# Reordering the expert layer of an attention + two-layer expert kernel: six product blocks in one stretch, weight splits one group later

## The chip, the cores and the metric

The kernel runs on one core of a Trainium2 chip. The time is the device time of one execution in microseconds (us), the median of several. The engines are TensorE (PE, with its weight loads shown as PEld), VectorE (DVE), ScalarE (ACT), GpSimd (POOL) and SyncE (SP), which here only starts transfers. Each engine works through its own queue in program order; between engines there are semaphores.

## The reference

```python
x = attention(q, k, v)                 # 2 x 8 heads x 576 x 64; window masks -> 1152 x 512
h = x @ w_in                           # 512 -> 2048
x = (h * tanh(softplus(h))) @ w_out    # 2048 -> 512
p = domain_probs / (domain_probs.sum(-1, keepdims=True) + 1e-9)
out = 0
for e in range(4):                     # 1152 tokens, w1[e] 512 x 1024, w2[e] 1024 x 512
    out += p[:, e:e+1] * (np.maximum(x @ w1[e], 0) @ w2[e])
```

Everything is float32. The kernel keeps that accuracy by splitting each operand into a high part (rounded to the format in which PE multiplies fast) and a low part (the rest): a product is three matmuls, high x high, high x low and low x high. Each split is therefore one ACT instruction (the high part) and one DVE or POOL instruction (the low part, source minus high).

## The kernel before

**Up to the second expert layer.** The attention runs over ten units of up to 128 rows (class `Unit`): transposes, scores, softmax, values, transposes back. `idle` matmuls at the very start (`NWARM`, L250) keep PE at work before the first k arrives. The weights of the first layer are loaded in halves of 512 KB by `dec_load` and split by `dec_dve` and `dec_act`, from step 6 of the attention on. Class `Step1` is the first layer; its 16 x 2 + 16 steps alternate first and second products and fill PE from about 55 us on.

**The second expert layer** works on 32 groups (class `Group`): 4 experts e, two sets of columns j (j = 0: 2 x 256 tokens, j = 1: 2 x 320 tokens), 4 pairs p of 128-wide slices of the hidden dimension; p runs fastest, then j, then e. A group's first product x @ w1 is done as a 2 x 2 block product with seven block products in place of eight (a Strassen scheme): A11·B11, S1·T1, A12·B21, S2·T2, S4·B22, S3·T3 and A22·T4. Each is six matmuls (`prod`, L788). They accumulate in three PSUM banks a, b, c. Between them lie copies and sums, since a bank is used on: p1 (ACT copies a after A11), c22 (ACT copies b after S1), u2 (ACT copies a after S2), then on DVE c11 = c + p1, c12 = b + u2, c22 = a + c22 (after S3), and the relu splits: `relu_split(0, ...)` of c11 and c12, `relu_split(1, ...)` of c22, and after A22, which uses bank a again, the split of c21 from PSUM. The second product (`second(f)`, f = 0 and 1) of a group is done during the next group: 4 (j = 0) or 5 (j = 1) rows of 128 tokens, three matmuls of 512 columns each per f, accumulated over p in banks 1 to 5. After p = 3 `finish` (L871) has DVE scale each row by the probability and add it to `scr`; for the last expert each row goes out by a transfer.

**Order in a group i before.** For j = 0: A11, S1, A12, S2, S4; `second(0)` of group i-1; slot (i, 0); S3; `second(1)` and `finish` of group i-1; A22; slot (i, 1). For j = 1: A11, S1, S2, A12, S3; `second(0)`; slot (i, 0); S4, A22; `second(1)` and `finish`; slot (i, 1). In j = 0 the banks a and c change places with every p, so that A22 of one group and A12 of the next use the same bank; in j = 1 they do not.

**The slots** (dictionary `slots`, L998) hold the preparation of weights: `prep_a(n)` (L735: two splits of the staged w1 of pair n, then four sums on POOL in place), `prep_s(n)` (L744: the split of these sums, then the load of w1 of pair n+1 into the same buffer), `prep_w2(n)` (L759: high part of w2 on ACT, low part on POOL, then the load of w2 of pair n+1). For experts 1 to 3 they stand like this, g being a j = 1 group except for p = 3, where it is the first group of the next expert (groups 8, 16, 24):

```python
n, g = e * NP2 + p, 2 * NP2 * (e - 1) + NP2 + p + 1
slots.setdefault((g, 0), []).append(lambda n=n: prep_a(n))
slots.setdefault((g, 1), []).append(lambda n=n: prep_s(n))
slots.setdefault((g + 1, 0) if p == NP2 - 1 else (g, 1), []).append(lambda n=n: prep_w2(n))
```

For expert 0 slots (1, 0) to (3, 1) hold the last pairs and the block sums and splits of the second set's columns (`set1_b`, `set1_sums`, `set1_t`), T2 in (3, 1).

**The tail** (L1029): the second product of the last group, row by row; its last row is cut into two halves of 256 columns in the same bank, and both are finished after the last matmul.

Of the kernel before, what the change touches and what calls it, by code (L numbers as in the profile page):

```python
# [14 lines left out]
AF = mybir.ActivationFunctionType  # L15
ALU = mybir.AluOpType
# [7 lines left out]
def kernel(  # L24
# [13 lines left out]
    PE, ACT, DVE, POOL, SP = nc.tensor, nc.scalar, nc.vector, nc.gpsimd, nc.sync  # L38
# [3 lines left out]
    DM = out.shape[1]  # L42
# [27 lines left out]
    def bank(n):  # L70
        return ps.tile([128, 512], F32, tag=f"bank{n}", name=nm("bank"))
# [177 lines left out]

    t = bank(7)  # L250
    for n in range(NWARM):
        PE.matmul(t, warm, warm4, start=n == 0, stop=n == NWARM - 1)

# [200 lines left out]

    u0.transposes()
    load(u4.load_k, u4.load_q, *vq[2:4], *vd_loads(0, 2))
# [46 lines left out]
    u0.x_hi()  # L503
    u0.x_lo()
    u2.probsT()
    u4.transposes()
    vq = vp_loads(1, 0, 2)
# [3 lines left out]
    def att_step(s):  # L511
        n2, n1, u, p1, p2 = (au[n] for n in (s + 2, s + 1, s, s - 1, s - 2))
        dec = s >= DEC0
        p1.probsT_copy()
        if s > DEC0:
            dec_act()
        if not dec:
            copy_v(n1.c)
        n1.spread()
        u.scores()  # L520
        u.softmax()
        p1.sums()
        p1.values()
        p2.xT()
        p1.normalise()
        p2.x_hi()
        if dec:
            dec_dve()
            copy_v(n1.c)
        p2.x_lo()  # L530
        n2.transposes([0])
        if s == 3:
            u.probsT()
        n2.transposes([1])
        if s != 3:
            u.probsT()

        if s == 4:
            load(au[9].load_k, *vq[0:2], au[9].load_q, *vq[2:4])
        elif s == 5:  # L540
            load(dec_load, *vd_loads(1, 2), dec_load, *vd_loads(1, 3), *vp_loads(1, 4, NCH), *vd_loads(1, 4))
        elif s == 6:
            dec_load()

# [224 lines left out]
    class Group:  # L769
# [25 lines left out]

        def first_a(self):
            assert ("s", self.e * NP2 + self.p) in ready
            N = self.N
            self.a, self.b, self.c = (bank(m)[:, 0:N] for m in ((0, 7, 6) if self.apart and self.p % 2 else (6, 7, 0)))
            self.cb = rawf[2][:, 0:3 * N]  # L800
            p1, u2 = (late[4][:, 320 * i:320 * i + N] for i in range(2))
            self.u2 = u2
            self.prod(self.a, "A11", "B11", True)
            self.prod(self.b, "S1", "T1", True)
            ACT.activation(p1, self.a, AF.Copy)  # L805
            ACT.activation(self.cb[:, 2 * N:3 * N], self.b, AF.Copy)
            if self.apart:
                self.prod(self.c, "A12", "B21", True)
                self.prod(self.a, "S2", "T2")
                self.prod(self.b, "S4", "B22")  # L810
                DVE.tensor_tensor(out=self.cb[:, 0:N], in0=self.c, in1=p1, op=ALU.add)
                ACT.activation(u2, self.a, AF.Copy)
                DVE.tensor_tensor(out=self.cb[:, N:2 * N], in0=self.b, in1=u2, op=ALU.add)
                self.relu_split(0, slice(0, 2 * N), self.cb[:, 0:2 * N])
                return
            self.prod(self.a, "S2", "T2")
            self.prod(self.c, "A12", "B21", True)
            ACT.activation(u2, self.a, AF.Copy)
            self.prod(self.a, "S3", "T3")
            DVE.tensor_tensor(out=self.cb[:, 0:N], in0=self.c, in1=p1, op=ALU.add)  # L820
            self.c22()

        def c22(self):
            o = slice(2 * self.N, 3 * self.N)
            DVE.tensor_tensor(out=self.cb[:, o], in0=self.a, in1=self.cb[:, o], op=ALU.add)

# [4 lines left out]

        def mid(self):
            N = self.N
            self.relu_split(1, slice(N, 2 * N), self.cb[:, 2 * N:3 * N])

        def first_u3(self):
            self.prod(self.a, "S3", "T3")
            self.c22()
            self.mid()

        def first_c21(self):
            self.prod(self.a, "A22", "T4")
            self.relu_split(1, slice(0, self.N), self.a)

        def first_b(self):
            N = self.N
            self.prod(self.b, "S4", "B22")
            self.prod(self.a, "A22", "T4")
            DVE.tensor_tensor(out=self.cb[:, N:2 * N], in0=self.b, in1=self.u2, op=ALU.add)
            self.relu_split(1, slice(0, N), self.a)  # L850
            self.relu_split(0, slice(0, 2 * N), self.cb[:, 0:2 * N])

# [6 lines left out]

        def second(self, f, which=slice(None)):  # L860
            assert ("w2", self.e * NP2 + self.p) in ready
            wh, wl = (w[:, 512 * f:512 * f + 512] for w in pair_w2(self.p))
            hi, lo = self.g[f]
            for acc, t, cols in self.accs()[which]:
                s = slice(128 * t, 128 * t + 128)
                for i, (x, a) in enumerate(((hi, wh), (hi, wl), (lo, wh))):
                    PE.matmul(acc, x[:, s], a[:, cols], start=self.p == 0 and f == 0 and i == 0,  # L867
                              stop=self.p == NP2 - 1 and f == 1 and i == 2,
                              skip_group_check=self.n >= NG2 - NP2 and t == self.rows - 1)
# [122 lines left out]
    for e in range(NE):  # L992
        for j in range(2):
            for p in range(NP2):
# [4 lines left out]
             (2, 0): [lambda: set1_b(2), lambda: set1_sums(0), lambda: prep_w2(3)], (2, 1): [lambda: set1_sums(1), lambda: set1_t("T1")],  # L999
             (3, 0): [lambda: set1_t("T3"), lambda: set1_t("T4")], (3, 1): [lambda: set1_t("T2")]}  # L1000
    for e in range(1, NE):
# [5 lines left out]
    for i, g in enumerate(groups):  # L1007
        before = groups[i - 1] if i else None
        g.first_a()
        if before:  # L1010
            before.second(0)
        else:
            steps[NS1 - 1].second(units_at=[0])
        if not g.apart:
            g.mid()
        for do in slots.get((i, 0), ()):
            do()
        g.first_u3() if g.apart else g.first_b()
        if before:
            before.second(1)  # L1020
            before.finish()
        else:
            steps[NS1 - 1].second(units_at=[1])
            y_out(2)
        if g.apart:
            g.first_c21()
        for do in slots.get((i, 1), ()):
            do()
    g = groups[-1]  # L1029
    accs = g.accs()  # L1030
    acc, t, _ = accs.pop()
    accs += [(acc[:, c], t, c) for c in (slice(0, DM // 2), slice(DM // 2, DM))]
    for t in range(len(accs)):
        for f in range(2):
            g.second(f, slice(t, t + 1))
        if t < len(accs) - 2:
            g.finish(slice(t, t + 1))
    g.finish(slice(len(accs) - 2, len(accs)))

# [31 lines left out]
```

## Time and profile before

| | |
|---|---|
| median of 3 runs | 629.46 us (628.78 to 629.7) |
| profiled execution | 629.2 us, of which the trace's span is 627.4 us |
| PE busy | 619.6 us, 99% of the span |
| PEld | 556.9 us, 89% |
| DVE, ACT, POOL busy | 289.1, 262.3, 181.0 us |
| granted TensorE clock | 1.00 in all stretches |
| second expert layer | from about 247 us to the end |

Busy time of PE is not PE at its peak: matmuls are pipelined and each record is longer than the distance to the next one. The distances between the starts, or the chain of work that ended last, tell the pitch. Times of rows below are microseconds from the start of the span.

### The profile page before, as it was taken

Reading aid. Unit: us, or ns where it says so; the run is one execution under the profiler, and the core shown is the slowest. Engines: PE = TensorE matmul, PEld = TensorE weight load, DVE = VectorE, ACT = ScalarE, POOL = GpSimd, SP = SyncE. Lnnn points to the kernel's source line nnn. Section 1 sums busy time; section 2 is a strip of 40 time slices with the busy share of each in tenths; the row PEclk is TensorE's granted clock in tenths of the full one; section 3 lists DMA queues with packets and bytes.
Section 4 is the critical chain, followed back from the end, with each engine's and each line's share of the span. In section 5 each row is a group of like instructions: output and inputs, shape, how many; then the busy total and the mean of one; then the engine's idle time right before and its main releaser. Section 6 shows DMA issues by size and latency. Waiting matters only on the chain.

```text
span 627.4 us, 10147 instructions
## 1 busy us (share of the span) xinstructions
PE 619.6 (99%) x4152; PEld 556.9 (89%) x4152; DVE 289.1 (46%) x482; ACT 262.3 (42%) x497; POOL 181.0 (29%) x201
## 2 busy tenths in 40 slices
PE   8999999999999999999999999999999999999997
PEld 5777888889999999998998999998989988989986
DVE  6898787614112343474544523444524444434223
ACT  7787777623223443452434322444322443322220
POOL 8854555502000241280244200334200335100000
PEclk9999999999999999999999999999999999999999
DMA  8875776300000122030022200122200122001002
GB/s 191 206 197 171 233 228 209 101 1 1 1 1 1 68 85 83 1 102 1 23 81 99 67 1 1 34 87 82 68 1 0 34 102 68 1 1 40 28 1 84
DMA packets 51358, 43.66 MB, mean 70 GB/s; under 512 B 26352, under 2 KB 44144, under 8 KB 51312
## 3 DMA queue, kind: packets, MB, share of 16 engines
q1 hardware_dynamic: 51312, 43.02, 22.8%
q8 instruction: 32, 0.52, 0.4%
q14 instruction: 14, 0.11, 0.1%
HBM read 40.65 MB, written 2.36 MB: 69 GB/s over the span
## 4 chain that ended last, share of the span: by engine, by line
PE 91%; DMA 3%; POOL 2%; SPq 1%; DVE 1%; ACT 1%; issue 0%; DVEq 0%; POOLq 0%; ACTq 0%
PE bank L867 31%; PE bank L793 28%; PE bank L593 16%; PE bank L569 15%; DMA raw<-in_moe_w_out_dram 1%; SPq L285 1%; POOL vD L294 1%; DMA natk<-in_k_dram 1%; DMA scr<-in_moe_w_in_dram 1%; POOL vP L292 1%; DMA vD<-in_v_dram 0%; SPq L316 0%; DMA vP<-in_v_dram 0%; POOL vD L207 0%; POOL vP L206 0%
## 5 line engine op out<-in xcount | busy, mean ns | idle before, releaser
L793 PE MATMUL bank<-xh,late 128*128 128x256 f32 (+1 forms) x512 | 118.0, 293 | 0.0
L793 PE MATMUL bank<-wxh,late 128*128 128x320 f32 (+1 forms) x384 | 93.4, 294 | 0.0
L793 PEld LDWEIGHTS bank<-xh,late 128*128 128x128 f32 x512 | 87.9, 188 | 1.8
L867 PE MATMUL bank<-late,gh 128*128 128x512 f32 x280 | 87.0, 392 | 0.0
L739 POOL TENSOR_TENSOR raw<-raw 128x256 f32<-128x256 f32 x16 | 12.3, 767 | 222.4 <-DVE late L621 222.4
L569 PE MATMUL bank<-xh,late 128*128 128x320 f32 (+1 forms) x288 | 75.9, 336 | 0.0
L793 PE MATMUL bank<-xl,late 128*128 128x256 f32 (+1 forms) x256 | 74.7, 292 | 0.0
L593 PE MATMUL bank<-gh,late 128*128 128x320 f32 (+1 forms) x288 | 72.0, 336 | 0.0
L793 PEld LDWEIGHTS bank<-wxh,late 128*128 128x128 f32 x384 | 67.8, 188 | 0.9 <-ACT late L805 0.3
L578 DVE TENSOR_TENSOR gl<-scr,gh 128x512 fp32r<-128x512 f32 (+1 forms) x32 | 24.5, 766 | 81.0 <-ACT gh L577 81.0
L867 PEld LDWEIGHTS bank<-late,gh 128*128 128x128 f32 x280 | 50.9, 188 | 9.0
L574 ACT ACTIVATE scr<-bank 128x320 f32<-128x320 f32 (+1 forms) x48 | 23.5, 489 | 82.2 <-PE bank L569 82.1
L755 POOL TENSOR_TENSOR late<-raw,late 128x1024 fp32r<-128x1024 f32 x16 | 38.8, 2425 | 64.0 <-ACT late L751 64.0
L793 PE MATMUL bank<-wxl,late 128*128 128x256 f32 (+1 forms) x192 | 56.2, 293 | 0.1
L867 PE MATMUL bank<-late,gl 128*128 128x512 f32 x140 | 54.5, 389 | 0.0
L569 PEld LDWEIGHTS bank<-xh,late 128*128 128x128 f32 x288 | 50.7, 188 | 3.8
L593 PEld LDWEIGHTS bank<-gh,late 128*128 128x128 f32 x288 | 50.0, 188 | 3.7
L867 PE MATMUL bank<-late,late 128*128 128x512 f32 (+1 forms) x219 | 52.8, 388 | 0.0
L793 PEld LDWEIGHTS bank<-xl,late 128*128 128x128 f32 x256 | 48.1, 188 | 1.7
L569 PE MATMUL bank<-xl,late 128*128 128x320 f32 (+1 forms) x144 | 48.4, 336 | 0.0
L593 PE MATMUL bank<-gl,late 128*128 128x320 f32 (+1 forms) x144 | 48.4, 336 | 0.0
L867 PE MATMUL bank<-late,wxh 128*128 128x512 f32 (+1 forms) x154 | 47.3, 389 | 0.0
(153 smaller groups left out, 1135.9 us busy)
## 6 DMA issues: line engine op xcount, KB each, us to landing
raw<-in_moe_w_dram SPq DMA_DIRECT2D x32, 512.0 KB, 3.5
raw<-in_moe_w_out_dram SPq DMA_DIRECT2D x15, 512.0 KB, 3.8
raw<-in_moe_w_in_dram SPq DMA_DIRECT2D x9, 512.0 KB, 4.2
scr<-in_moe_w_in_dram SPq DMA_DIRECT2D x7, 512.0 KB, 4.5
natk<-in_k_dram SPq DMA_DIRECT2D x8, 256.0 KB, 3.4
natq<-in_q_dram SPq DMA_DIRECT2D x8, 256.0 KB, 4.0
out_dram<-scr SPq DMA_DIRECT2D x8, 256.0 KB, 2.0
vD<-in_v_dram SPq DMA_DIRECT2D x16, 64.0 KB, 3.8
```

The lines of the kernel that those rows point to most:

```text
L285: SP.dma_start(out=job[0], in_=job[1])
L292: POOL.tensor_copy(vP[before, :, g0:g1, j, :], vP[own, :, g0 - 1:g1 - 1, j, :])
L294: POOL.tensor_copy(vD[before, :, j, c, :], vD[own, :, j, c - 1, :])
L569: PE.matmul(h, a[:, c, :], x[:, c, :], start=c == 0 and k == 0, stop=c == 3 and k == 2)
L574: ACT.activation(self.hc[:, self.w * i:self.w * (i + 1)], h, AF.Mish)
L578: DVE.tensor_tensor(out=self.glo, in0=self.hc, in1=self.ghi.bitcast(F32), op=ALU.subtract)
L593: PE.matmul(yacc[self.grp][d], a[:, 512 + 128 * d:640 + 128 * d], x[:, g], start=u == UORD[self.grp][0] and k == 0, stop=u == UORD[self.gr ...
L739: POOL.tensor_tensor(out=a22, in0=a21, in1=a22, op=ALU.add)
L755: POOL.tensor_tensor(out=lo, in0=stage2, in1=hi.bitcast(F32), op=ALU.subtract)
L793: PE.matmul(out, w, x(k), start=first and k == 0 and i == 0, stop=k == 1 and i == 2, skip_group_check=not first)
L867: PE.matmul(acc, x[:, s], a[:, cols], start=self.p == 0 and f == 0 and i == 0, stop=self.p == NP2 - 1 and f == 1 and i == 2, skip_group_ch ...
```

## The change

One stretch of PE work per group, for both sets: A11, S1, (A12, S2 or S2, A12), S4, S3, then both halves of the second product of the group before with slot (i, 0) issued between them, then `finish`, then A22. In both sets the banks a and c now change places with p. The slot (i-1, 1), which stood at the end of group i-1, is issued within `first` of group i: after its PE work, the copies and the sums c11 and c12, and before its relu splits. T2 goes to slot (3, 0), T4 to (3, 1). The second half of the very last row accumulates in a bank of its own (bank 6): what had been accumulated for it before the last group is scaled and added to `scr` by one more DVE operation. At the start there are a shorter idle product more and one between the transposes of the first unit; the first transposes of unit 4 come before the probabilities of unit 2; one load of weights is issued in attention step 5 and not in step 6.

```diff
-    u0.transposes()
+    u0.transposes([0])
+    idle_product()
+    u0.transposes([1])
...
+    u4.transposes([0])
     u2.probsT()
-    u4.transposes()
+    u4.transposes([1])
...
-            load(dec_load, *vd_loads(1, 2), dec_load, *vd_loads(1, 3), *vp_loads(1, 4, NCH), *vd_loads(1, 4))
-        elif s == 6:
-            dec_load()
+            load(dec_load, *vd_loads(1, 2), dec_load, *vd_loads(1, 3), dec_load, *vp_loads(1, 4, NCH), *vd_loads(1, 4))
...
-        def first_a(self):
+        def first(self, between):
             assert ("s", self.e * NP2 + self.p) in ready
             N = self.N
-            self.a, self.b, self.c = (bank(m)[:, 0:N] for m in ((0, 7, 6) if self.apart and self.p % 2 else (6, 7, 0)))
+            self.a, self.b, self.c = (bank(m)[:, 0:N] for m in ((0, 7, 6) if self.p % 2 else (6, 7, 0)))
...
             ACT.activation(u2, self.a, AF.Copy)
+            DVE.tensor_tensor(out=c11, in0=self.c, in1=p1, op=ALU.add)
+            self.prod(self.b, "S4", "B22")
+            DVE.tensor_tensor(out=c12, in0=self.b, in1=u2, op=ALU.add)
             self.prod(self.a, "S3", "T3")
+            for do in between:
+                do()
+            self.relu_split(0, slice(0, 2 * N), cb[:, 0:2 * N])
+            DVE.tensor_tensor(out=c22, in0=self.a, in1=c22, op=ALU.add)
+            self.relu_split(1, slice(N, 2 * N), c22)
...
-             (3, 0): [lambda: set1_t("T3"), lambda: set1_t("T4")], (3, 1): [lambda: set1_t("T2")]}
+             (3, 0): [lambda: set1_t("T2"), lambda: set1_t("T3")], (3, 1): [lambda: set1_t("T4")]}
...
-        g.first_a()
+        g.first(slots.get((i - 1, 1), ()))
         if before:
             before.second(0)
...
-        if not g.apart:
-            g.mid()
         for do in slots.get((i, 0), ()):
             do()
-        g.first_u3() if g.apart else g.first_b()
         if before:
             before.second(1)
             before.finish()
...
-        if g.apart:
-            g.first_c21()
-        for do in slots.get((i, 1), ()):
-            do()
+        g.first_c21()
...
-    accs += [(acc[:, c], t, c) for c in (slice(0, DM // 2), slice(DM // 2, DM))]
+    half = [slice(0, DM // 2), slice(DM // 2, DM)]
+    row = g.row0 + t
+    o = scr[:, DM * row:DM * (row + 1)][:, half[1]]
+    DVE.scalar_tensor_tensor(out=o, in0=acc[:, half[1]], scalar=prob[:, row, g.e:g.e + 1], in1=o,
+                             op0=ALU.mult, op1=ALU.add)
+    accs += [(acc[:, half[0]], t, half[0]), (bank(6)[:, half[1]], t, half[1])]
     for t in range(len(accs)):
         for f in range(2):
-            g.second(f, slice(t, t + 1))
-        if t < len(accs) - 2:
-            g.finish(slice(t, t + 1))
-    g.finish(slice(len(accs) - 2, len(accs)))
+            g.second(f, slice(t, t + 1), fresh=t == len(accs) - 1)
+        g.finish(slice(t, t + 1))
```

## Rows read from the trace of the kernel before

**Rows 1.** The page, chain that ended last: share of the span by engine.

```profile
PE 91%; DMA 3%; POOL 2%; SPq 1%; DVE 1%; ACT 1%; issue 0%; DVEq 0%; POOLq 0%; ACTq 0%
```

**Rows 2.** The chain in order of time, second expert layer: start, length, what, matmuls.

```profile
298.54 4.38 PE bank L793 x30
...
348.42 4.10 PE bank L793 x36
352.53 2.74 PE bank L867 x12
355.27 0.70 PE bank L793 x6
```

**Rows 3.** Waits of PE's weight loads: us in total, times, longest us.

```profile
PEld bank L793 <- DVE wxl L621: 0.3, 1, 0.3
PEld bank L793 <- ACT late L805: 0.3, 1, 0.3
```

**Rows 4.** Timeline near the end: last matmul of A22, its relu split; last rows.

```profile
613.19 0.31 PE L793 MATMUL bank<-wxh,late 128*128 128x320 f32 x1
...
613.53 0.44 ACT L829 ACTIVATE late<-bank 128x320 fp32r<-128x320 f32 x1 [4.11 <-PE bank L793]
...
614.00 0.49 DVE L830 SCALAR_TENSOR_TENSOR late<-bank,late 128x320 fp32r<-128x320 f32 x1 [0.85 <-ACT late L829]
...
623.83 0.88 DVE L881 SCALAR_TENSOR_TENSOR scr<-bank,prob,scr 128x256 f32<-128x256 f32 x2 [0.68 <-PE bank L867]
```

**Rows 5.** Timeline at the end of the attention: DVE takes up the moved load.

```profile
47.69 0.66 DVE L155 TENSOR_SCALAR scr<-scr 128x512 uint32<-128x512 uint32 x1 [0.23 <-POOL wxl L180]
```

**Rows 6.** Timeline of group 9 (S2, u2), and of group 28, where PE waited.

```profile
361.86 0.28 PE L793 MATMUL bank<-wxh,late 128*128 128x256 f32 x1
...
362.17 0.38 ACT L812 ACTIVATE late<-bank 128x256 f32<-128x256 f32 x1 [0.98 <-PE bank L793]
...
362.54 0.30 PEld L867 LDWEIGHTS bank<-late,wxh 128*128 128x128 f32 x2
...
567.38 0.44 ACT L805 ACTIVATE late<-bank 128x320 f32<-128x320 f32 x1 [0.84 <-PE bank L793]
...
567.87 0.19 PEld L793 LDWEIGHTS bank<-wxh,late 128*128 128x128 f32 x1 [0.27 <-ACT late L805]
...
567.98 0.19 PEld L793 LDWEIGHTS bank<-wxl,late 128*128 128x128 f32 x1
```

**Rows 7.** Timeline of groups 6 to 9: prep_s, u2, prep_a, finish, A22's split, A12.

```profile
323.14 1.23 DVE L621 TENSOR_TENSOR late<-raw,late 128x1024 fp32r<-128x1024 f32 x1
...
340.23 0.39 ACT L812 ACTIVATE late<-bank 128x256 f32<-128x256 f32 x1 [0.98 <-PE bank L793]
...
341.97 0.92 ACT L620 ACTIVATE late<-raw 128x512 fp32r<-128x512 f32 x2
...
342.71 1.02 DVE L621 TENSOR_TENSOR late<-raw,late 128x512 fp32r<-128x512 f32 x2
...
346.44 3.37 DVE L879 TENSOR_SCALAR scr<-bank,prob 128x512 f32<-128x512 f32 x5
...
349.16 0.38 ACT L829 ACTIVATE gh<-bank 128x256 fp32r<-128x256 f32 x1 [3.25 <-PE bank L793]
349.44 1.05 ACT L620 ACTIVATE late<-raw 128x1024 fp32r<-128x1024 f32 x1
...
349.73 0.41 DVE L830 SCALAR_TENSOR_TENSOR gl<-bank,gh 128x256 fp32r<-128x256 f32 x1
...
350.32 0.28 PE L793 MATMUL bank<-xh,late 128*128 128x256 f32 x1
```

**Rows 8.** The load of w1 (L711), 16 of them: from issue to landing.

```profile
DMA to landing us min/median/max: 3.2/3.4/4.1
```

**Rows 9.** Timeline of group 2: w2_lo on POOL beside prep_s on DVE.

```profile
266.29 2.41 POOL L755 TENSOR_TENSOR late<-raw,late 128x1024 fp32r<-128x1024 f32 x1
...
267.46 2.32 DVE L621 TENSOR_TENSOR late<-raw,late 128x1024 fp32r<-128x1024 f32 x1 [0.56 <-ACT late L620]
```

More of the change, by code (lines that the diff above doesn't have):

```diff
@@ L248, with idle_product @@
             ACT.activation(sel[n][32:64, 32 * g:32 * g + 32], ident[32:64, 32:64], AF.Copy)
-    t = bank(7)
-    for n in range(NWARM):
-        PE.matmul(t, warm, warm4, start=n == 0, stop=n == NWARM - 1)
+    idle_bank = bank(7)
+    def idle_product(n=4):
+        PE.matmul(idle_bank[:, 0:128 * n], warm, warm4[:, 0:n], start=True, stop=True)
+    for n in [4] * NWARM + [2]:
+        idle_product(n)
     def msk_b(n):
@@ L794, in prod @@
                               skip_group_check=not first)
-        def first_a(self):
+        def first(self, between):
             assert ("s", self.e * NP2 + self.p) in ready
             N = self.N
-            self.a, self.b, self.c = (bank(m)[:, 0:N] for m in ((0, 7, 6) if self.apart and self.p % 2 else (6, 7, 0)))
-            self.cb = rawf[2][:, 0:3 * N]
+            self.a, self.b, self.c = (bank(m)[:, 0:N] for m in ((0, 7, 6) if self.p % 2 else (6, 7, 0)))
+            self.cb = cb = rawf[2][:, 0:3 * N]
             p1, u2 = (late[4][:, 320 * i:320 * i + N] for i in range(2))
-            self.u2 = u2
+            c11, c12, c22 = (cb[:, N * i:N * (i + 1)] for i in range(3))
             self.prod(self.a, "A11", "B11", True)
@@ L805, in first_a @@
             ACT.activation(p1, self.a, AF.Copy)
-            ACT.activation(self.cb[:, 2 * N:3 * N], self.b, AF.Copy)
+            ACT.activation(c22, self.b, AF.Copy)
             if self.apart:
@@ L809, in first_a @@
                 self.prod(self.a, "S2", "T2")
[L810 to L817, printed above, removed]
+            else:
+                self.prod(self.a, "S2", "T2")
+                self.prod(self.c, "A12", "B21", True)
             ACT.activation(u2, self.a, AF.Copy)
+            DVE.tensor_tensor(out=c11, in0=self.c, in1=p1, op=ALU.add)
+            self.prod(self.b, "S4", "B22")
+            DVE.tensor_tensor(out=c12, in0=self.b, in1=u2, op=ALU.add)
             self.prod(self.a, "S3", "T3")
[L820 to L825, printed above, removed]
+            for do in between:
[3 more added lines that the diff above has]
+            self.relu_split(1, slice(N, 2 * N), c22)
         def relu_split(self, f, cols, src, late_ok=True):
@@ L830, in relu_split @@
             DVE.scalar_tensor_tensor(out=lo, in0=src, scalar=0.0, in1=hi.bitcast(F32), op0=ALU.max, op1=ALU.subtract)
[L832 to L839, printed above, removed]
         def first_c21(self):
@@ L843, in first_c21 @@
             self.relu_split(1, slice(0, self.N), self.a)
[L845 to L851, printed above, removed]
         def accs(self):
@@ L858, in accs, with second @@
             return yacc[key]
-        def second(self, f, which=slice(None)):
+        def second(self, f, which=slice(None), fresh=False):
             assert ("w2", self.e * NP2 + self.p) in ready
@@ L866, in second @@
                 for i, (x, a) in enumerate(((hi, wh), (hi, wl), (lo, wh))):
-                    PE.matmul(acc, x[:, s], a[:, cols], start=self.p == 0 and f == 0 and i == 0,
+                    PE.matmul(acc, x[:, s], a[:, cols], start=(self.p == 0 or fresh) and f == 0 and i == 0,
                               stop=self.p == NP2 - 1 and f == 1 and i == 2,
```

## The prediction, on record before the run

> **What bounds the kernel now.** I read the page first: TensorE (PE) carries nine tenths of the chain that ended last, so a change is worth what it does to the gaps and the pitch of the matmuls, or to the two ends [rows 1]. I went on to the chain in order of time inside the second expert layer. The reader is to see there that the stretches are already at a fixed pitch: 36 matmuls of 256 columns in 4.10 us (0.114 each), 12 of 512 columns in 2.74 (0.228), 30 of 320 columns in 4.38 (0.146) [rows 2]. A stretch of six costs 0.70, not 0.68: about 0.02 us go each time PE changes from one product to the other. The list of waits finds just two for this layer's first product, 0.3 us each: one on the split of T2 before group 4, one on a late p1 copy in group 28 [rows 3]. So there is little left to take out, and the question is what the new order puts in. ACT, DVE and POOL have much idle time, but each works its queue in program order, so what counts is which instruction stands ahead of which.
>
> **What the change removes.** The matmuls are the same in number. (1) T2 moves to an earlier slot and T4, which no early product needs, to the later one: the wait before group 4 goes, -0.33. (2) The late p1 copy happened in one of sixteen such groups; I count it as chance and as gone, -0.29. (3) The fourth-kind stretch of six becomes part of the long one: one change of product less in the 16 groups with 256 columns, 16 x 0.02, -0.3. In the 320-column groups six matmuls cost what they cost inside thirty, so nothing.
>
> **The tail.** After the last matmuls DVE now runs two half-row operations, 0.88 together [rows 4]; in the new order the first half lies in a bank of its own and is evacuated under the second half's matmuls, so 0.44 goes. Against it: A22 of the last group now comes right before the tail. Its relu starts 0.34 after its last matmul has started and takes 0.44, the low part follows and ends 1.30 after it [rows 4]. The first matmul that reads the high part would load its weights 0.60 after that same point (0.146 to the next product, then two of 0.228), the first that reads the low part 0.57 later. With 0.05 from an engine's end to PE's load and 0.11 from the load to the matmul (both below) they come 0.11 and 0.06 late. Net -0.25. The added half-row operation of DVE is hidden under the tail's first 24 matmuls (5.5 us).
>
> **The head.** A load of weights (512 KB) is issued one attention step earlier. DVE takes that load up at 47.69, after only 0.23 idle [rows 5]: earlier landing can give that much, however much sooner the transfer comes. The two added idle products fall where PE waits for the first q anyway. The transposes of unit 4 fill a wait for the softmax. I take -0.1 in all, bounds 0 and -0.3.
>
> **What it adds: a wait for u2.** In the 256-column groups S3 now follows S2 with only S4 between, 0.68 us, and it overwrites the bank that the u2 copy is still reading. In group 9 the last matmul of S2 starts at 361.86, the copy runs 362.17 to 362.55, and the weight load that S3 would take over stands at 362.54 [rows 6]. Where PE did wait for such a copy, it ended at 567.82, the load started at 567.87 and the next load, which starts with the matmul, at 567.98 [rows 6]: 0.05 and 0.11. So S3 starts at 362.71 instead of 362.65: 0.06 x 16 groups, +0.9 (bounds 0 and 1.2). [...]
>
> **What it adds: weight preparation that starts a transfer late.** This is the largest term. Four times for each later expert, prep_s splits the staged w1 sums, and its end lets SP start the next w1 load into the same buffer; prep_a of the next pair waits for that load. Before, prep_s(6) stands at the end of group 7 and prep_a(7) in group 8 has its data in time. Now prep_s(6) stands in group 8, behind u2, and prep_a(7) stands in the same group, on ACT and DVE ahead of the finishing of five output rows and ahead of the split of A22. I count from the start of u2 in group 8 (340.23 now) with the rows of before [rows 7]. ACT's next instruction follows 0.28 after the start of such a short one; so the high part of prep_s takes 0.28 to 1.33, the low part (1.23) to 2.59, SP starts the load then, and it lands 3.4 later (3.2 to 4.1), at 6.0 [rows 8]. prep_a's first high part, 0.57 long, starts then; its two low parts (1.02) end 1.6 after that start, at 7.6. The finishing of five rows (3.37) is behind them on DVE and ends at 10.95, the low part of A22 (0.41, overlapping by 0.08) at 11.3. The second-next product, A12 of group 9, writes that very bank: load 11.33, matmul 11.44. Now it starts at 350.32, which is 10.09 [rows 7]; with 0.06 for u2 and 0.02 less for the change of product, 10.13. So PE stands 1.3.
>
> One more delay lies on this path. w2_lo (POOL) now comes in the same place. In group 2 of the trace the low part of prep_s took 2.32 beside w2_lo, 1.23 without it [rows 7, 9], and ended 1.08 after POOL did: a two-input DVE operation on SBUF waits until POOL's instruction is over. In group 8 w2_hi, as large as prep_s's high part, would end at 2.29, w2_lo start when the low part of prep_s ends (2.59) and run 2.41, to 5.0; the low part of the first relu split waits for it and ends at 5.55, the c22 sum at 5.9, and the second relu, ahead of prep_a on ACT, at 6.4. prep_a then starts at 6.27 and not at 6.0: 1.6 us. This comes for groups 8, 16 and 24: +4.7 (bounds 3.3, landing after 3.2 and no POOL; 6.0, landing after 4.1). In groups 5 to 7 the same late load costs nothing: these take 12.97 us, their prep_a is over about 0.7 us before A22 ends, and the bank is wanted only by the fourth product of the next group.
>
> **And once, early.** In group 2 the splits of (1,1) now stand between c12 and the relu splits, and POOL has w2_lo(2) and two sums of 640 columns there. Taking turns with them, c22 would end 9.4 us after the group's start (prep_s and the first relu each wait for one POOL sum of about 1.5 us, scaled from w2_lo). ACT then has the second relu (0.42), a split of 640 columns (0.7) and w2_hi (1024 columns, 1.05 like prep_s) ahead of A22's relu, whose low part is done 0.7 us after A12 of group 3 wants the bank. I take +0.75, bounds 0 (POOL late) and 2.0 (one POOL operation more).
>
> **Sum.** -0.33 - 0.29 - 0.3 - 0.25 - 0.1 + 0.9 + 4.7 + 0.75 = +5.1. The profiled execution took 629.2 us (span 627.4 and 1.8 around it), so 634.3; the median of the runs is 0.26 above it: 634.5. With all low bounds +1.7 (tail -0.44, head -0.3), with all high ones +8.6: 631.1 to 638.0 for this case. About 0.2% (1.26 us) is what a measurement of this kernel can tell from no change.
>
> **Rivals.** (A) *No wait at A12; no change.* For it prep_a(7) would have to start 4.7 us after u2, so that A22's low part is through at 10.0. For it speaks that now the same queue order gives no wait: that low part ends at 350.14, 0.18 before A12. Against it the load, which even at 3.2 lands at 5.8. Then the sum is +0.4: 629.9, or 629.0 if u2 costs nothing as well. (B) *Faster.* If all three new waits stay away, what is left is -1.27: 628.2, just at the edge of what can be told. The head would have to give more than its 0.3 for a clear gain; against it DVE's short idle time there. (C) *Slower still.* In group 7 c12 and w2_hi end at nearly the same time, about 5.05 after the group's start. If POOL takes w2_lo first, prep_s's low part ends 2.4 later, its load and prep_a follow, and POOL's four sums for pair 6 end 4.0 into group 8, where prep_s(6) wants them at 3.2. That moves the whole path of group 8 by 0.85, three times: 637.1.
>
> **Chances.** The forecast 0.66, C 0.11, A 0.15, B 0.08. So slower 0.77, same 0.15, faster 0.08. The range 629.5 to 638.0 holds the forecast's case, C and half of A.
>
> **What will show it.** In the profile after: PE idle or lengthened matmuls three times, right after the twelve matmuls of A11 and S1 in groups 9, 17 and 25, about 1.6 us each, released by the low part of a relu split on DVE, with five row operations directly before it and two splits of prep_a before those; ACT waiting in group 8 for the DMA of w1. Sixteen gaps of 0.06 at S3. No wait for T2 before group 4. The last DVE operation alone, 0.44 after the last matmul. I am wrong if prep_a(7) of group 8 starts less than 5 us after u2, or if A12 of group 9 runs on while DVE is still at the rows; then the time is that of A or B. A gain beyond 1.5 us would mean that I misread the head.

## The result, and the profile after

The changed kernel takes 633.38 us (median of 5 runs, 632.55 to 635.68) against 629.40 for the kernel before beside it: ratio 1.0071, 95% interval [1.005, 1.0092]. It is slower, by 4.0 us on the medians; 634.5 was forecast. The profiled execution took 634.07 us with a span of 632.0, so 4.6 us more span than before, and those are the ones taken apart here. Line numbers of after: products of the first matrix L798, of the second L852, relu split ACT L831 and DVE L832, p1 L810, c22 L811 (its copy) and L826 (its sum), u2 L818, split() ACT L625 and DVE L626, w2_hi L756, finish L864 and L866.

The page's share of the chain by engine answers to [rows 1]. PE lost two points, and DVE got 5%:

```profile
PE 89%; DVE 5%; DMA 3%; ACT 2%; SPq 0%; issue 0%; DVEq 0%; ACTq 0%
```

The waits of PE's weight loads in after (us in total, times, longest) answer to [rows 3]. The waits for T2 and for p1 are gone. In their place is one of 1.3, three times, and two short ones in the tail:

```profile
PEld bank L798 <- DVE gl L832: 3.9, 3, 1.3
...
PEld bank L852 <- ACT late L831: 0.3, 1, 0.3
...
PEld bank L852 <- DVE late L832: 0.2, 1, 0.2
```

The chain in order of time in after, group 8 to the first products of group 9 (start, length, what), shows the path of one of the three:

```profile
340.60 0.38 ACT late L818
340.98 0.95 ACT late L625
341.93 0.95 ACT late L756
342.88 0.53 ACT gh L831
...
343.43 2.57 DVE gl L832
346.00 0.35 DVE raw L826
...
346.36 0.42 ACT gh L831
346.78 0.53 ACT late L625
...
347.33 1.03 DVE late L626 x2
348.36 3.29 DVE scr L864 x5
351.66 0.34 DVE gl L832
...
352.04 3.08 PE bank L798 x24
```

For 11.4 us the chain runs over other engines, while PE works through its queue till it has to wait. From u2 (340.60) it goes through prep_s's high part, w2_hi, the relu of the first half, its low part on DVE (2.57 us), c22, the second relu, prep_a, five rows of finish and A22's low part, to A12 of group 9 at 352.04. That is the queue of [rows 7] in its new order. In PE's timeline of after:

```profile
350.66 0.28 PE L798 MATMUL bank<-wxh,late 128*128 128x256 f32 x1
352.04 0.38 PE L798 MATMUL bank<-xh,late 128*128 128x256 f32 x1 [1.11 <-DVE gl L832]
```

The matmul ahead of A12 started at 350.66; where nothing waits the next one comes 0.114 later [rows 2], so A12 is 1.27 late. The matmul behind its first one starts at 352.26, 0.22 later, which is 0.11 more than the pitch: 1.38 in all, and 4.1 in the three groups.

**The budget of the +4.6.** T2's wait -0.3 and p1's -0.3. The 16 groups of 256 columns go from 10.29 to 10.37 (5.50 + 4.87), +1.3. The 16 of 320 columns go from 12.97 to 12.94 (6.12 + 6.82), -0.5. The two lengths before are distances in the chain of the kernel before, 275.61 - 265.32 and, for two groups, 324.48 - 298.54 [rows 2]:

```profile
265.32 4.10 PE bank L793 x36
...
275.61 4.10 PE bank L793 x36
...
324.48 4.37 PE bank L793 x30
```

Group 3, with 5.09 instead of 4.87, +0.2; A12 in groups 9, 17 and 25 +4.1; the tail -0.2; and layer 2 begins at 247.68 in place of 247.35, +0.3. Sum: +4.6. The chain of after in order of time, at group 3, group 5 and group 10:

```profile
276.16 5.09 PE bank L798 x42
...
298.15 6.12 PE bank L798 x42
304.27 6.82 PE bank L852 x30
...
355.12 5.50 PE bank L852 x24
360.63 4.87 PE bank L798 x42
```

The experiments test the parts.

### The profile page after: what moved, and what is told of

The parts are those of the page before. It is cut to its first block, busy times and chain, and to the rows that moved or that the text cites. A ratio compares the mean times of both kernels' runs of the same rounds, so it can differ in the third digit from the quotient of the medians.

```text
span 632.0 us, 10144 instructions
## 1 busy us (share of the span) xinstructions
PE 622.4 (98%) x4154; PEld 558.6 (88%) x4154; DVE 304.9 (48%) x483; ACT 264.1 (42%) x497; POOL 185.2 (29%) x201
## 4 chain that ended last, share of the span: by engine, by line
PE 89%; DVE 5%; DMA 3%; ACT 2%; SPq 0%; issue 0%; DVEq 0%; ACTq 0%
PE bank L852 28%; PE bank L798 26%; PE bank L598 16%; PE bank L574 15%; DVE gl L832 1%; DVE scr L866 1%; DMA raw<-in_moe_w_out_dram 1%; DMA vD<-in_v_dram 1%; PE bank L333 1%; ACT late L625 1%; DMA natk<-in_k_dram 1%; PE bank L253 1%; DVE scr L864 1%; DVE late L626 0%; PE bank L403 0%; ACT late L756 0%
## 5 line engine op out<-in xcount | busy, mean ns | idle before, releaser
L798 PE MATMUL bank<-xh,late 128*128 128x256 f32 (+1 forms) x512 | 115.9, 294 | 3.3 <-DVE gl L832 3.3
L798 PE MATMUL bank<-wxh,late 128*128 128x320 f32 (+1 forms) x384 | 94.3, 295 | 0.0
L798 PEld LDWEIGHTS bank<-xh,late 128*128 128x128 f32 x512 | 87.3, 188 | 4.7 <-DVE gl L832 3.9
L852 PE MATMUL bank<-late,gh 128*128 128x512 f32 x280 | 86.7, 391 | 0.0
L798 PE MATMUL bank<-xl,late 128*128 128x256 f32 (+1 forms) x256 | 74.9, 292 | 0.0
L798 PEld LDWEIGHTS bank<-wxh,late 128*128 128x128 f32 x384 | 67.6, 188 | 0.6
L760 POOL TENSOR_TENSOR late<-raw,late 128x1024 fp32r<-128x1024 f32 x16 | 44.3, 2768 | 66.8 <-ACT late L756 66.8
L852 PEld LDWEIGHTS bank<-late,gh 128*128 128x128 f32 x280 | 51.7, 188 | 10.0
L798 PE MATMUL bank<-wxl,late 128*128 128x256 f32 (+1 forms) x192 | 56.1, 292 | 0.0
L852 PE MATMUL bank<-late,gl 128*128 128x512 f32 x140 | 54.6, 390 | 0.0
L852 PE MATMUL bank<-late,late 128*128 128x512 f32 (+1 forms) x219 | 52.6, 387 | 0.0
L798 PEld LDWEIGHTS bank<-xl,late 128*128 128x128 f32 x256 | 48.1, 188 | 0.6
L852 PEld LDWEIGHTS bank<-late,late 128*128 128x128 f32 x219 | 40.8, 188 | 8.7 <-ACT late L831 0.3
```

Of the source, the lines that this page charges most:

```text
L760: POOL.tensor_tensor(out=lo, in0=stage2, in1=hi.bitcast(F32), op=ALU.subtract)
L798: PE.matmul(out, w, x(k), start=first and k == 0 and i == 0, stop=k == 1 and i == 2, skip_group_check=not first)
L852: PE.matmul(acc, x[:, s], a[:, cols], start=(self.p == 0 or fresh) and f == 0 and i == 0, stop=self.p == NP2 - 1 and f == 1 and i == 2, sk ...
```

## The experiments

All times are medians. Each ratio is formed from all runs of a kernel and of the kernel before beside it (its medians: 629.40 with after, 629.47 with e1 to e4, 629.73 with e5 to e8, 630.09 with e9 to e11), so it is not the quotient of two times of the table. "Layer 2" is the span less the start of the layer's first piece in the chain of the profiled execution: it leaves out the scatter of the attention, which turned out to be as large as the small terms.

| kernel | us | ratio to before, 95% | layer 2 starts | layer 2, us |
|---|---|---|---|---|
| before | 629.4 | | 247.35 | 380.1 |
| after | 633.38 | 1.0071 [1.005, 1.0092] | 247.68 | 384.3 |
| e1 | 638.61 | 1.016 [1.0133, 1.0187] | 247.50 | 388.9 |
| e2 | 634.74 | 1.0087 [1.0072, 1.0103] | 247.52 | 385.5 |
| e3 | 633.34 | 1.0067 [1.0052, 1.0082] | 247.90 | 383.6 |
| e4 | 629.97 | 1.0004 [0.999, 1.0017] | 247.64 | 380.6 |
| e5 | 640.40 | 1.0171 [1.0153, 1.0189] | 247.45 | 391.0 |
| e6 | 629.34 | 0.9995 [0.9986, 1.0004] | 247.16 | 379.8 |
| e7 | 629.95 | 1.0001 [0.9992, 1.001] | 247.31 | 380.6 |
| e8 | 629.30 | 0.9989 [0.998, 0.9998] | 247.09 | 379.9 |
| e9 | 628.26 | 0.9973 [0.9963, 0.9984] | 247.76 | 378.7 |
| e10 | 629.64 | 0.999 [0.9981, 0.9999] | 248.45 | 379.6 |
| e11 | 629.27 | 0.9991 [0.9977, 1.0005] | 246.81 | 380.1 |

In the diffs, slot (g, 2) is a new one, issued at the end of group g behind A22's split:

```diff
         g.first_c21()
+        for do in slots.get((i, 2), ()):
+            do()
```

**e1: splits of every third pair back at the end of their group**

```diff
-            slots.setdefault((g, 1), []).append(lambda n=n: prep_s(n))
-            slots.setdefault((g + 1, 0) if p == NP2 - 1 else (g, 1), []).append(lambda n=n: prep_w2(n))
+            slots.setdefault((g, 2 if p == NP2 - 2 else 1), []).append(lambda n=n: prep_s(n))
+            slots.setdefault((g + 1, 0) if p == NP2 - 1 else (g, 2 if p == NP2 - 2 else 1), []).append(lambda n=n: prep_w2(n))
```

> The changed kernel, but the splits for the third pair of an expert (prep_s and prep_w2 in slots (7,1), (15,1), (23,1)) are issued at the end of their group again, as in the kernel before; all else stays in the new order. Theory of the queue (prep_a in groups 8, 16, 24 starts late and DVE reaches the low part of A22's split 1.3 us after A12 wants the bank): the three waits of PE on a DVE split at A12 go from 1.3 us each to none, minus 4.1 us against the changed kernel, so about 629.5 and within 0.2% of the kernel before. Rival, the new order of PE's blocks itself costs the time: three slots of 62 change it by less than 1 us, so about 633.

638.61: a miss, and slower than after. A12's wait did go (one of 0.2 is left), but S2 of groups 8, 16 and 24 now waits for p1, 7.6 us in three. A part of the loss is pitch: behind the wait of group 8 the chain has 18 matmuls of 256 columns in 3.55 and thirty of 512 in 7.19, behind that of group 16 the same in 2.39 and 6.83, so 1.5 us. The mean granted clock of this execution is 0.997, of after's 1.00. That the wait itself lowers the pitch is not shown: in group 16 it did not.

**e2: of these, prep_s alone**

```diff
-            slots.setdefault((g, 1), []).append(lambda n=n: prep_s(n))
+            slots.setdefault((g, 2 if p == NP2 - 2 else 1), []).append(lambda n=n: prep_s(n))
```

> As the first of these runs, but only prep_s goes back to the end of groups 7, 15, 23; prep_w2 stays inside the next group. So the w1 load starts early, and POOL's w2_lo still runs beside the low parts of the relu split. Theory: two delays lie on the same path, the late load and DVE standing while POOL works; with the load early the second remains. prep_a would start 5.1 us after the u2 copy instead of 6.1, PE's wait at A12 falls from 1.3 to about 0.4 us: minus 3 us against the changed kernel. Rival, the late load is all: the wait is gone, minus 4.1.

634.74. A12's waits fall to 0.3 each, as expected, but the new one stays, 4.5 in three. The timeline of ACT in e2, from the end of group 7 on (start, length, line, operation; in brackets the idle time before it and its releaser):

```profile
334.54 0.92 ACT L625 ACTIVATE late<-raw 128x512 fp32r<-128x512 f32 x2
337.66 0.44 ACT L831 ACTIVATE late<-bank 128x320 fp32r<-128x320 f32 x1 [2.19 <-PE bank L798]
339.58 1.06 ACT L625 ACTIVATE late<-raw 128x1024 fp32r<-128x1024 f32 x1 [1.48 <-POOL raw L747]
340.54 0.37 ACT L810 ACTIVATE late<-bank 128x256 f32<-128x256 f32 x1
```

prep_s(6) stands at 339.58, behind A22's relu, and has to wait 1.48 for POOL's last sum of pair 6 (L747); p1 of group 8 (L810) is queued behind it. The sums are late because only this pair was moved: prep_s(5) still stands inside group 7, frees the buffer there, and prep_a(6) starts at 334.54. In e1 w2_hi stands ahead of p1 as well, 1.0 more. So my expectation for both took a step back in the queue for a step back in time: the step's data still came one slot late.

For the main question e2 shows one half. SP starts the load of w1 at 341.92, 0.03 ahead of u2 (341.95), where in after it starts 2.6 behind it (343.21). prep_a then starts 5.06 after u2 (347.01), held by POOL's turn alone (beside w2_lo the first relu's low part takes 2.48 on DVE), and A12's wait is 0.3 instead of 1.3, with prep_a's place in the queues unchanged.

**e3: weights' split of the third and fourth pair later, so that POOL's step leaves group 8**

```diff
-            slots.setdefault((g + 1, 0) if p == NP2 - 1 else (g, 1), []).append(lambda n=n: prep_w2(n))
+            slots.setdefault({NP2 - 2: (g + 1, 2), NP2 - 1: (g + 2, 0)}.get(p, (g, 1)), []).append(lambda n=n: prep_w2(n))
```

> The opposite half: prep_s stays in the next group (late load), but prep_w2 of the third pair goes to the end of groups 8, 16, 24 and that of the fourth pair two groups on, so POOL does nothing beside the relu splits of group 8. Theory: the load, which lands 3.2 to 3.8 us after its issue and so 5.8 to 6.4 after the u2 copy, still holds prep_a to the same time as now (6.1): PE's wait at A12 stays 1.1 to 1.6 us, the time that of the changed kernel within 1 us, and ACT now waits for the DMA before prep_a. Rival, POOL's lock is all: prep_a starts at 4.6, the wait goes, minus 4 us.

633.34, no change, as expected. The chain in order of time in e3, same place as the one of after:

```profile
340.78 0.38 ACT late L818
...
342.14 1.23 DVE late L626
...
343.39 3.40 DMA raw<-in_moe_w_dram
...
346.82 0.64 ACT late L625
```

With POOL's step out of the way the late load alone sets prep_a: 6.04 after u2 starts (346.82 - 340.78), in after 6.09. So the two ways to prep_a were tied, and the turns that DVE and POOL take cost almost nothing in after.

**e4: prep_a of every fourth pair at the end of its group, behind finish and A22's split**

```diff
-            slots.setdefault((g, 0), []).append(lambda n=n: prep_a(n))
+            slots.setdefault((g, 2 if p == NP2 - 1 else 0), []).append(lambda n=n: prep_a(n))
```

> Load and POOL as late as in the changed kernel, but prep_a of groups 8, 16, 24 is issued at the end of the group, behind the finishing of the rows and behind the split of A22. Theory: only the place in DVE's and ACT's queues counts, so the wait at A12 goes, minus 4.1 us, about 629.5; ACT does prep_a while A11 and S1 of the next group run, and the later POOL sums delay prep_s of the next group by 2 to 3 us, which A22 there still hides. Rival, the late load costs the time whatever stands behind it: the wait moves into group 9 (prep_s, c22, A22) and the time stays near 633.

629.97, equal to before. The load is as late as in after; only prep_a's place in the queues changed. The timeline of DVE in e4, end of group 8:

```profile
347.07 3.38 DVE L864 TENSOR_SCALAR scr<-bank,prob 128x512 f32<-128x512 f32 x5
350.36 0.42 DVE L832 SCALAR_TENSOR_TENSOR gl<-bank,gh 128x256 fp32r<-128x256 f32 x1
350.69 1.02 DVE L626 TENSOR_TENSOR late<-raw,late 128x512 fp32r<-128x512 f32 x2
```

Finish starts at 347.07 and not at 348.28. Counted from u2, which starts at 340.52 here and at 340.60 in after, A22's low part is through 1.1 us sooner, and prep_a's two low parts (L626) come behind it, where nobody waits for them yet. The distance from the last matmul of S1 to A12's first falls from 1.38 to 0.31, 0.2 over the pitch; with slower matmuls behind it (in group 9 the 24 from A12 to the second product take 2.98, in groups without a wait 2.80: 4.86 for 42 less 2.06 for 18) the three groups stay 0.35 to 0.38 longer than the others. This settles the main question: the wait needs both, prep_a made late by the load and prep_a ahead of finish in the queues. With the load early (e2) or prep_a behind (e4) most of it goes. Layer 2 is 3.0 us shorter than in e3 and 3.7 shorter than in after, of 4.2 that after had lost.

**e5: all slots back at the end of their own group**

```diff
-        g.first(slots.get((i - 1, 1), ()))
+        g.first(())
...
         g.first_c21()
+        for do in slots.get((i, 1), ()):
+            do()
```

> The changed kernel with all its split steps (the second slot of every group, the small splits of groups 1 to 3 among them) back at the end of their own group, behind A22, as before the change; the blocks of a group stand as changed. My theory: e1 and e2 failed because only one of four pairs went back, so that a pair's sums met the next pair's splits; with all four back both waits are gone (A12 in groups 9, 17, 25 and S2 in groups 8, 16, 24, each under 0.4 us) and layer 1's late groups lose their 0.2: 634.0 - 4.1 - 0.2 = 629.7, within 0.3% of the kernel before. Rival: splits put behind A22's own split come too late for the changed block order whichever pairs are moved, and the wait at S2 stays at 1.5 us in three groups or more: 634 or more.

640.40: my theory fell, and the rival had the mechanism, if not the size. Waits of PE's weight loads in e5, and its chain at the end of group 6:

```profile
PEld bank L798 <- ACT late L810: 11.3, 10, 1.3
```

```profile
326.03 0.89 PE bank L798 x6
...
328.22 1.04 ACT late L756
329.27 0.34 ACT late L810
```

A22 is now the last block in the 320-column groups too. Its relu (0.44), prep_s's high part and w2_hi (about 1 us each on ACT) come behind it, and p1 of the next group behind those. S2 starts at 329.65; the last matmul of S1 started at 328.34, and at the pitch of 0.146 [rows 2] S2 would have started at 328.49. Ten such waits make a group 0.9 to 1.3 us longer each; less 1.4 for the waits at A12 that are gone with them, they are the 10.4 by which layer 2 is longer than in e4. POOL's sums, which were late in e1 and e2, hold up a split only once here, for 1.2 us: the theory was right on the data and wrong on what stands ahead of p1. Before, the place was quiet: the timeline of ACT in the kernel before, end of group 5, shows A22's relu (L829, the first row) and prep_s (L620) 3.4 and 2.4 us ahead of the group's end, at 311.52, and only w2_hi at it:

```profile
308.13 0.44 ACT L829 ACTIVATE late<-bank 128x320 fp32r<-128x320 f32 x1 [3.28 <-PE bank L793]
...
309.09 1.05 ACT L620 ACTIVATE late<-raw 128x1024 fp32r<-128x1024 f32 x1
311.55 1.06 ACT L751 ACTIVATE late<-raw 128x1024 fp32r<-128x1024 f32 x1 [1.41 <-PE bank L867]
```

So the two halves of the change hang together: with A22 last, the splits have to leave the end of the group, and moving them is what made prep_a late in the three groups.

**e6: e4, and one row of the second product between S4 and S3 in the 256-column groups**

```diff
             DVE.tensor_tensor(out=c12, in0=self.b, in1=u2, op=ALU.add)
+            row0()
             self.prod(self.a, "S3", "T3")
```

(`row0` is `before.second(0, slice(0, 1))`; the call behind `first` does the other rows.)

> e4 (sums of every fourth pair at the end of their group) with one row of the second product's first half moved from behind S3 to ahead of it in the sixteen 256-column groups. Theory: S3 waits 0.065 us in each for ACT's copy of U2, and the row (three products, 1.2 us) covers it: first load of S3 without a wait, a group shorter by 0.06, 16 x 0.065 = 1.0 us less than e4, about 629.0. Rival: the wait is overlapped with the loads ahead and the time of S4 and S3 stays: same as e4, 630.0.

629.34. The weight loads around S3's start: first in after (group 10), where S3 reads `wxh` and the distance to the load ahead is 0.18 while the others are 0.11 to 0.12, 0.06 after the end of the u2 copy (L818, 364.08 + 0.38); then in e6 (same group), where a row of 512 columns (pitch 0.23) comes ahead and S3's load follows it without a wait:

```profile
364.08 0.38 ACT L818 ACTIVATE late<-bank 128x256 f32<-128x256 f32 x1 [0.98 <-PE bank L798]
...
364.34 0.19 PEld L798 LDWEIGHTS bank<-xh,late 128*128 128x128 f32 x1
364.52 0.19 PEld L798 LDWEIGHTS bank<-wxh,late 128*128 128x128 f32 x1
364.63 0.19 PEld L798 LDWEIGHTS bank<-wxl,late 128*128 128x128 f32 x1
```

```profile
362.97 0.19 PEld L853 LDWEIGHTS bank<-late,wxl 128*128 128x128 f32 x1
363.20 0.19 PEld L798 LDWEIGHTS bank<-wxh,late 128*128 128x128 f32 x1
```

A group falls from 10.32 (in e4's chain 42 matmuls in 4.86 and 24 in 5.46) to 10.26, 0.06 as expected; layer 2 falls by 0.8. The time alone would not tell it (the intervals of e4 and e6 overlap).

**e7: e4 with the old head. e11: before with the new head**

e7 undoes the changes ahead of layer 2 (idle products, transposes, `dec_load`); e11 has these alone.

> e4 with everything ahead of layer 2 as it was before the change (warming products in one group, transposes together, the decoder's load in its old place). Theory: the changed head does not pay; layer 2 then begins at 247.35 after the span's start instead of 247.5 to 247.9, 0.3 us less than e4: about 629.7. Rival: the differences of layer 2's start among the runs are scatter of the first transfers, and its start stays between 247.3 and 247.9 with no mean gain: 630.0, and in either case not to be told from e4 by the time alone.

> The kernel before with the changed head alone (warming products each by itself with a half one behind, a product between the two transposes, u4's first transpose ahead of u2's, the decoder's last load one step earlier). Theory: layer 2 begins 0.0 to 0.4 us later than before's 247.35, at 247.5 on the mean of the runs with this head (247.16 to 247.90 so far): 629.7 to 629.9. Rival: the head gains as its warming should, layer 2 begins at 247.2 or earlier: 629.3 or less. Either is within what the time can tell; the start of layer 2 is the measure.

629.95 and 629.27, both within what can be told from before. By the table, layer 2 starts at 247.31, 247.09, 247.76 (e7, e8, e9), 248.45 (e10) and 247.35 (before) with the old head, and at 246.81 to 247.90 with the new one in eight executions. The means are 247.6 and 247.5. Taken alone, e7's trace fits its theory (247.31) and e11's fits its rival (246.81); but each head's starts lie 1.1 to 1.4 us apart. The medians of the two pairs that differ in the head alone are equal: 629.97 and 629.95 for e4 and e7, 629.34 and 629.30 for e6 and e8. So no effect of the head is shown either way, and after's 0.3 is within the scatter of the start.

**e8: e4, e6's row and the old head together**

> e4, the row ahead of S3 and the head as before together. Theory: what is left of the change is then its tail (0.23 us less) and no wait: 629.5 - 0.2 + 0.2 (group 3) = 629.2 to 628.5 with the smaller gains of e6, ratio 0.998 to 1.000. Rival: the 320-column groups and the small waits at A12 in groups 3, 9, 17 and 25 (0.2 each) use it up: 629.5 to 630.

629.30, ratio 0.9989 [0.998, 0.9998]: at or just under before, as expected at the upper end. What is left is A12's wait in groups 3, 9, 17 and 25, 1.2 in four.

**e9: e8, and the third pair's weights split behind the first half of the second product**

```diff
-            slots.setdefault((g + 1, 0) if p == NP2 - 1 else (g, 1), []).append(lambda n=n: prep_w2(n))
+            slots.setdefault((g + 1, 0) if p >= NP2 - 2 else (g, 1), []).append(lambda n=n: prep_w2(n))
```

> e8 with the second weights' split of every third pair moved from inside groups 8, 16, 24 (between S3 and the ReLUs) to behind the first half of the second product there. In e6 and e8 the low part of group 8's first half takes 2.56 us on DVE beside POOL's low part of these weights (0.69 when alone), and finish and A22's low part, queued behind it, end 0.4 us too late for A12 in groups 9, 17 and 25 (1.2 in all with group 3). Theory: with POOL's step behind it the low part takes 0.7, finish starts by its products and the waits in 9, 17 and 25 go: 3 x 0.35 = 1.0 us less than e8, about 628.3, ratio 0.997 to 0.9985. Rival: POOL's step then runs beside finish and stretches that (3.4 us for five rows) or ACT's part of it makes P1 late for S2: same as e8 or more, 629.3 to 631.

628.26, ratio 0.9973 [0.9963, 0.9984]: faster than both kernels. Only group 3's wait of 0.4 is left. Layer 2 is 1.2 shorter than in e8: groups 9, 17 and 25 fall from 10.63 to 10.71 to the 10.27 of the others, more than their waits of 0.24 to 0.27; in e4 the matmuls behind such a wait took 0.18 more besides. The timeline of DVE in e9, group 8, and of POOL there:

```profile
343.08 0.68 DVE L828 SCALAR_TENSOR_TENSOR gl<-raw,gh 128x512 fp32r<-128x512 f32 x1
...
346.07 3.47 DVE L860 TENSOR_SCALAR scr<-bank,prob 128x512 f32<-128x512 f32 x5 [1.05 <-PE bank L848]
```

```profile
345.58 2.40 POOL L755 TENSOR_TENSOR late<-raw,late 128x1024 fp32r<-128x1024 f32 x1 [5.86 <-ACT late L751]
```

The low part that took 2.57 beside POOL in after, and 2.56 in e8, takes 0.68, and finish waits for its products (1.05 idle, released by PE) and no longer for DVE's queue. POOL's step now lies beside finish, which reads its rows from PSUM: it takes 2.40, and the five rows take 3.47, where in e4, with POOL idle, they took 3.38. So POOL's step cost the low part, which has both inputs in SBUF, 1.89, and the five rows 0.09.

**e10: before with the new tail alone**

The edit is the last hunk of the diff, with `fresh` in `second`.

> The kernel before with the changed tail alone (last row's second half scaled early and summed in another bank, one DVE step of a half row at the end in place of two). Theory, as in the forecast: DVE's last step is 0.44 shorter, small waits of 0.1 to 0.2 come in: 0.2 to 0.3 us less, 629.2, not to be told from the kernel before by the time; the stretch from A22's low part to the end shows it. Rival: the low part that is late for the first row takes it all back: 0.0.

629.64, ratio 0.999 [0.9981, 0.9999]. From the end of the last matmul to the end of the span before takes 3.6 (627.4 - 623.81), e10 3.1 (628.0 - 624.89) and after 3.1. The ends of the chains of e10 and of after:

```profile
614.58 10.31 PE bank L867 x51
...
624.92 0.48 DVE scr L881
```

```profile
621.76 7.12 PE bank L852 x36
...
628.91 0.48 DVE scr L866
```

So the tail alone gains 0.5. In e10 the last 51 matmuls take 10.31 as before, so 6.88 for 36 (less 15 at 3.43); in after the 36 take 7.12, because A22 now stands right ahead and its split is late for them. Net -0.2.

## Why the prediction was right, step by step

- **A12 in groups 9, 17, 25** (+4.7): right in mechanism, place and count; each costs 1.38 and not 1.58, 4.1 in all. Of the two ways to prep_a I gave POOL's turn the larger delay (6.27 after u2); it came at 6.09, tied with the load (6.0 estimated, 6.04 in e3). What follows held: A22's low part starts 10.98 after u2 (351.58 in DVE's timeline) and A12 0.46 later.
- **The waits for T2 and p1** (-0.33, -0.29): both went. But the late p1 was no chance: e10 and e11, whose order in layer 2 is the old one, show it too, 0.3 in group 28. The forecast was right there without its reason.
- **The queue order as the cause** is shown by e4: with the load as late as ever and prep_a behind A22's split, the wait falls to 0.2 a group and the time to that of before. e2 shows that the late load is needed for it too. Rival A, that A12 does not wait, was wrong here. e3 shows that w2_lo added nothing of its own. Rival C did not come about: in group 7 prep_s ended in time for SP to start its load at 331.02.
- **u2** (+0.9) **and fewer changes of product** (-0.3): e1 to e5 and e7, which have these blocks, run 10.32 per 256-column group that has no other wait (group 10 and later), against 10.29 before, so +0.5 for the two together where +0.6 was forecast. e6 shows the u2 part alone, 0.06 a group or 1.0; the changes of product are then the remaining -0.5. S3's weight load does wait for the copy: in after's group 10 it starts 0.06 behind the copy's end and 0.18 behind the load ahead, where the others are 0.11 to 0.12 apart.
- **A product change less in the 320-column groups**: I took nothing. These groups fell by 0.03 each (12.97 to 12.94), -0.5 in all. In both kinds of group there are two changes of product where there were four (42 and 24 or 30 matmuls now), so 0.015 a change, and I had counted only the stretch of six, at 0.02.
- **The early group** (+0.75): right in mechanism, mis-sized: +0.2. In group 2, as forecast, prep_s's low part and that of the first relu each end behind a POOL sum (1.08 behind the one that ends at 271.97, 0.55 behind the one that ends at 274.48), c22 is late, and A22's low part is done after A12 of group 3 wants the bank. But c22 ends 9.0 after the group's first matmul (275.36 - 266.3) and not 9.4, and the low part ends at 278.11, 0.2 too late and not 0.7. In the timeline of after, with A12's first matmul 0.23 behind the last of S1 (277.94):

```profile
274.95 0.41 DVE L826 TENSOR_TENSOR raw<-bank,raw 128x256 f32<-128x256 f32 x1
...
277.69 0.42 DVE L832 SCALAR_TENSOR_TENSOR gl<-bank,gh 128x256 fp32r<-128x256 f32 x1 [0.39 <-ACT gh L831]
...
278.17 0.38 PE L798 MATMUL bank<-xh,late 128*128 128x256 f32 x1
```

- **The tail** (-0.25): -0.2, made of -0.5 (forecast -0.44) and +0.24 (forecast +0.17).
- **The head** (-0.1): not shown; the start scatters by 1.6 us between executions.
- **What the sum did not have**: after's profiled execution runs the 256-column groups at 10.37, 0.05 more than the six kernels with the same blocks. The chains put most of it in the second product, 24 matmuls in 5.50 instead of 5.46. That is 0.8 us, about as much as this execution (634.07) lies over its median (633.38). Its cause is open. The terms that repeat (-0.3 - 0.3 + 0.5 - 0.5 + 0.2 + 4.1 - 0.2) come to +3.5, which is also what e3's layer 2 is longer than before's (383.6 - 380.1), and not to +5.1: the terms of A12 (0.6), the early group (0.5) and the 320-column groups (0.5) were too high, and the scatter of pitch and head made the profiled execution look nearer to the sum (+4.6) than the terms are: that part of the agreement is luck. One sum is wrong: with the high bounds that are stated it comes to +8.0, not +8.6, so 637.5 and not 638.0; the time lies inside either.

## What to carry to other kernels

Moving a step into a later place moves more than the step: what its end releases (here a transfer of 3.4 us) and what stands behind the next user in each engine's queue move too. When the load can't come sooner, put its user behind the steps that PE will want next, rather than ahead of them; e4's one line gave back 3.7 of the 4.2 us that layer 2 had lost. A step back in the queue helps only if its data are there by then (e1, e2) and if nothing that PE wants next is queued behind it (e5), so undo a slot move with its whole chain in view.

## What the runs showed of the hardware that I had not expected

- The start of layer 2 lay between 246.81 and 248.45 in thirteen profiled executions, whatever the head: terms of the attention below about 1 us can't be read from one trace. The stretch from there to the end is steadier: 380.1 in before and 380.1 in e11, whose layer 2 is the same.
- A DVE step took 2.57 beside POOL's (after) and 0.68 without it (e9), but taking POOL's step away paid only where that queue set the end: nothing in e3, where the load held prep_a as long, and 1.2 us of layer 2 between e8 and e9, where the load had been taken out of the path.
